# A Fourier layer in front of a mixture of experts: the first forward step in one full-precision matmul, an earlier first table, and the inverse's copies in another place of the queues

## The chip, the cores and the metric

The kernel runs on one core of one Trainium2 chip. Its time is the device time in microseconds of one execution. Five engines work side by side, each on a queue of its own that it takes in order: TensorE (PE, with its weight loads shown as PEld), VectorE (DVE), ScalarE (ACT), GpSimd (POOL) and SyncE (SP), which here only issues DMAs.

## The reference

A batch of 8 sequences of 2496 tokens of 256 numbers goes through a real Fourier transform along the sequence, a complex 256 x 256 product with a bias, a soft threshold and the inverse transform; each of the 19968 tokens then goes to the one of 8 experts that its gate scores highest.

```python
X = np.fft.rfft(x, axis=1)
Yr = Xr @ w_r - Xi @ w_i + b_r
Yi = Xr @ w_i + Xi @ w_r + b_i
Yr = np.sign(Yr) * np.maximum(np.abs(Yr) - lam, 0.0)   # Yi likewise
y = np.fft.irfft(Y, n=x.shape[1], axis=1)
# per token, with its expert e = argmax(y @ w_gate):
out = softmax(y @ w_gate)[e] * (np.maximum(y @ w1[e], 0.0) @ w2[e])
```

## The kernel before

**Numbers.** Where precision matters and speed too, a factor is split: a copy rounded to a reduced form (fp32r) on ScalarE, the rest by a subtraction on VectorE, and a product is three matmuls in the reduced form, high by high, low by high and high by low. Some matmuls take full-precision float32 instead.

**The transform** of 2496 = 39 x 64 is done in steps. The first forward step `fwd_a` (L279) multiplies a block of x by a 117 x 120 matrix of cosines and sines; a batch is 11 blocks, two for each of five x tiles and one for the sixth. Batch 0 uses float32 and one matmul a block (tile `pa`, from `x` and `far` or `fer`); the others use three, from `xh` and `xl`, which `split_x` (L269) makes. The result is copied to `ae` and stored in memory (`spec`), and `turn` (L300) loads it back turned, as `t`. Then come ten slots a batch, two frequencies of the 20 in each: `fwd_b` (L307) writes `pb`; `halves` (L317) makes `re`, `sh`, `su`, `sl` of it; `mix` (L333) makes the products `pk` and, behind it, `pm`, with `k` copied on ScalarE, `kb` added on GpSimd and `v` added on VectorE; `shrink` (L358) makes `r` on ScalarE and `y` on VectorE. The inverse of a batch runs in the slots of the next: `inv_b` (L374) makes `pv` and copies it to `z`, and `inv_a` (L387) makes `pz`, the split `zh` and `zl`, then `py`, copied to `yb`.

**The routing.** When half of a batch's `yb` is there, `route` (L558) chooses the expert of each token and its row in a sorted buffer `xs`. It is a generator: each `tick` (L519) runs it on to its next `yield`, so that its small VectorE steps are strewn over the slots. It makes a running sum, `sb`, which TensorE multiplies into `pr`; four ticks lie between them. Its rows are then scattered by GpSimd (L624), three a slot, four in the last batch, by `send` (L524). `table` (L638), also run by ticks, turns the counts into a list of tiles of 256 tokens. The first table serves the first 5 tiles, the second all others.

**The loop** is `spectral` (L411), from L454 on, over 80 slots. It enters ScalarE's and VectorE's instructions in the order written; TensorE's and SyncE's are written by hand as well. A slot `it` of batch b, slot number s, goes: `fwd_b` of the next slot, the first part of its `halves`, `r` of the slot before, the last part of `halves`, ticks, an inverse, `mix` and `fwd_a`, `y`, `split_x` for the next slot's `fwd_a`, ticks, an inverse, `y`, ticks, `pm` and `v`, an inverse, ticks, sends, DMA loads. In slots 2 to 5 of each batch but the first ("turning") three steps of `inv_a` run, one in each inverse, and `fwd_a` stands in front of `pk`; in the others the inverse is `inv_b`. `first` and `second` say which blocks a slot takes, `loads` which x tile it loads: in batch 2 and later the loads lie three or more slots ahead of use.

**Behind the loop** `finish_last` (L531) runs the last batch's `inv_a` and routing beside the first three steps of the experts (`step`, L899; `up`, L830; `down`, L859), in which `split1` and `split2` split the weights; then `experts_rest` runs the others.

Of the kernel before, what the change touches and what calls it, by code (L numbers as in the profile page):

```python
# [24 lines left out]
D = 256  # L25
# [73 lines left out]
class Kernel:  # L99
    def __init__(self, tc, nb, x, w_r, w_i, b_r, b_i, w_gate, w1, w2,  # L100
                 c_fa, c_fe, c_ga, c_bm, c_bi, c_ids, c_score, c_base, c_ltri, c_tcol, out):
        self.__dict__.update({n: v for n, v in locals().items() if n != "self"})
        self.nc = tc.nc
        self.ntok = nb * S
        self.cap = TT + self.ntok
        self.nt = (self.ntok + E * (TT - 1)) // TT
        done = (nb - 1) * S
        self.early = EARLY if done - E * (TT - 1) > (EARLY - 1) * TT else 0
        self.spec = [self.nc.dram_tensor(f"spec{i}_dram", (120, G, D), F32, kind="Internal").ap() for i in range(2)]
        self.xs = self.nc.dram_tensor("xs_dram", (E * self.cap, XW), F32, kind="Internal").ap()  # L110
# [69 lines left out]
    def open_forward(self, st):  # L180
        tc, nc, nb = self.tc, self.nc, self.nb
        f = self.f = self.pool(st, "f", 1, side="right")
        self.xp = self.pool(st, "xp", 5, side="right")
        self.tp = self.pool(st, "tp", 6, side="right")
        self.w = self.pool(st, "w", 2, side="right")
        self.psf = self.pool(st, "psf", 1, side="right", space=PSUM)

        self.far = far = f.tile([117, 120], F32, name="far")
        self.fh = f.tile([117, 120], F32R, name="fh")
        self.fl = f.tile([117, 120], F32R, name="fl")  # L190
        self.fer = f.tile([78, 120], F32, name="fer")
        self.feh = f.tile([78, 120], F32R, name="feh")
        self.fel = f.tile([78, 120], F32R, name="fel")
        nc.sync.dma_start(far, self.c_fa)
        nc.sync.dma_start(self.fer, self.c_fe)
        self.bm = f.tile([128, K1, 128], F32, name="bm")
        self.bi = f.tile([128, K1, 128], F32, name="bi")
        self.bias = f.tile([128, 2, D], F32, name="bias")
        self.xg = {}
        for q in range(6):  # L200
            self.load_x(0, q)
        nc.sync.dma_start(self.bm[:, 0:4, :], self.c_bm[:, 0:4, :])
        raw = {}
        for nm, src in (("r", self.w_r), ("i", self.w_i)):
            raw[nm] = self.w.tile([128, 2, D], F32, tag="v", name="wraw")
            nc.sync.dma_start(raw[nm], src.rearrange("(c p) n -> p c n", p=128))
        self.wh, self.wl = {}, {}
        self.raw = raw
        for h, b in ((0, self.b_r), (1, self.b_i)):
            nc.gpsimd.dma_start(self.bias[:, h, :], b.rearrange("(o n) -> o n", o=1).broadcast_to((128, D)))  # L210
        self.nlam = f.tile([128, 1], F32, name="nlam")
        nc.vector.memset(self.nlam, -LAM)

        nc.gpsimd.dma_start(self.gar, self.c_ga)
        for c in range(2):
            nc.gpsimd.dma_start(self.iw[:, c, c * 128:c * 128 + 8], self.w_gate[c * 128:(c + 1) * 128, :])
        nc.gpsimd.dma_start(self.ids, self.c_ids)
        nc.gpsimd.dma_start(self.score, self.c_score)
        nc.gpsimd.dma_start(self.base, self.c_base)
        nc.gpsimd.dma_start(self.ltri_f, self.c_ltri)  # L220
        nc.gpsimd.dma_start(self.tcol, self.c_tcol)
        nc.gpsimd.memset(self.z[:, :, 64:66, :], 0.0)
# [12 lines left out]

    def split_constants(self):
        nc, f, raw = self.nc, self.f, self.raw
        nc.scalar.copy(self.fh, self.far)
        nc.vector.tensor_sub(self.fl, self.far, self.fh)
        nc.scalar.copy(self.feh, self.fer)  # L240
        nc.vector.tensor_sub(self.fel, self.fer, self.feh)
        ws = self.w.tile([128, 2, D], F32, tag="r", name="wsum")
        wd = self.w.tile([128, 2, D], F32, tag="r", name="wdif")
        nc.vector.tensor_sub(wd, raw["i"], raw["r"])
        nc.vector.scalar_tensor_tensor(out=ws, in0=raw["i"], scalar=-1.0, in1=raw["r"], op0=ALU.mult, op1=ALU.subtract)
        raw = {"r": raw["r"], "d": wd, "s": ws}
        for nm in ("s", "d", "r"):
            self.wh[nm] = f.tile([128, 2, D], F32R, name="wh" + nm)
            self.wl[nm] = f.tile([128, 2, D], F32R, name="wl" + nm)
            nc.scalar.copy(self.wh[nm], raw[nm])  # L250
            nc.vector.tensor_sub(self.wl[nm], raw[nm], self.wh[nm])
        nc.scalar.copy(self.gh, self.gar)
        nc.vector.tensor_sub(self.gl, self.gar, self.gh)
        for c in range(2):
            nc.vector.tensor_copy(self.iw[:, c, 8 - 8 * c:136 - 8 * c], self.ident)
        nc.vector.tensor_copy(self.ltri, self.ltri_f)
# [9 lines left out]
            self.nc.sync.dma_start(t[lo * j:hi * j, :n, :].rearrange("p g d -> p (g d)"), src)  # L266
        self.xg[b, q] = t

    def split_x(self, b, q, g):  # L269
        nc = self.nc  # L270
        m = 117 if q < 5 else 78
        xt = self.xg[b, q][:m, g:g + 2, :].rearrange("p g d -> p (g d)")
        xh = self.w.tile([117, 512], F32R, tag="xh", name="xh")
        xl = self.w.tile([117, 512], F32R, tag="xl", name="xl")
        nc.scalar.copy(xh[:m, :], xt)  # L275
        nc.vector.tensor_sub(xl[:m, :], xt, xh[:m, :])  # L276
        self.xs2[b, q, g] = xh, xl

    def fwd_a(self, b, q, g):  # L279
        nc = self.nc  # L280
        m = 117 if q < 5 else 78
        raw, hi, lo = (self.far, self.fh, self.fl) if q < 5 else (self.fer, self.feh, self.fel)
        p = self.psi.tile([128, 512], F32, tag="u", name="pa", bufs=4)
        if b:
            xh, xl = self.xs2.pop((b, q, g))
            parts = ((hi, xh), (lo, xh), (hi, xl))
        else:
            parts = ((raw, self.xg[b, q][:, g:g + 2, :].rearrange("p g d -> p (g d)")),)
        for i, (a, v) in enumerate(parts):
            nc.tensor.matmul(p[:120, :], a[:m, :], v[:m, :], start=i == 0, stop=i == len(parts) - 1)  # L290
        ae = self.xp.tile([120, 2, D], F32, tag="ae", name="ae", bufs=5)
        to = ae.rearrange("p g d -> p (g d)")
        if b == 0 and g:
            nc.vector.tensor_copy(to, p[:120, :])
        else:
            with self.tc.high_priority():
                nc.scalar.copy(to, p[:120, :])
        nc.sync.dma_start(self.spec[b % 2][:, 4 * q + g:4 * q + g + 2, :], ae)
# [111 lines left out]

    def spectral(self, fwd):  # L411
        nb = self.nb
        self.t1s, self.pbs, self.ss, self.us, self.ys, self.hl, self.xs2 = {}, {}, {}, {}, {}, {}, {}
        self.jobs, self.rows = [], []
        pairs = [(q, g) for q in range(6) for g in ((0, 2) if q < 5 else (0,))]
        todo = [(b, s) for b in range(nb) for s in range(10)]
# [17 lines left out]
        for _ in self.halves(*todo[0]):  # L434
            pass

        first, second, loads, back = ({i: [] for i in range(-1, n)} for _ in range(4))
        for b in range(1, nb):
            at = 10 * b - 10
            for i, o in enumerate((1, 1, 2, 2, 3, 3, 4, 4, 5, 5, 6) if b == 1 else (-3, -2, -1, 0, 0, 1, 2, 3, 4, 5, 6)):  # L440
                first[at + o].append((b, *pairs[i]))
                second[at + o - 1].append((b, *pairs[i]))
            for q, o in enumerate((None, None, 0, 1, 1, 2) if b == 1 else (-7, -5, -4, -2, 0, 2)):
                if o is not None:
                    loads[at + o].append((b, q))
# [8 lines left out]
        for it in range(n):  # L454
            b, s = todo[it]
            late = b == nb - 1
            half, small = iter(()), iter(())
            if it + 1 < n:
                self.fwd_b(*todo[it + 1])
                half = self.halves(*todo[it + 1])  # L460
                next(half)
            if it:
                small = self.shrink(*todo[it - 1])
                next(small)
            next(half, None)
            turning = b and 2 <= s < 6
            turns = iter(range(3 * s - 6, 3 * s - 3) if turning else ())

            def inverse():
# [4 lines left out]
                    break  # L474

            spare = 1 if late else 0
            self.tick(2 + spare)
            inverse()
            mix = self.mix(b, s)
            if not turning:  # L480
                next(mix)
# [2 lines left out]
            if turning:  # L484
                next(mix)
            next(small, None)
            for a in second[it]:
                self.split_x(*a)
            self.tick(2 + spare)
            inverse()  # L490
            next(small, None)
# [8 lines left out]
                self.write_blank()  # L500
            if it + 4 < n:
                self.turn(*todo[it + 4])
            if late and self.early and s == 6:
                self.jobs.append(self.table(0))
        for _ in self.shrink(*todo[n - 1]):
            pass
# [51 lines left out]
    def route(self, b, hf, y):  # L558
# [39 lines left out]
        pa = pa[:, 8:, :]  # L598
        sb = small("sb", (117, E), BF16)
        nc.vector.tensor_copy(sb, pa[:, GH - 1, :])  # L600
        for _ in range(4):
            yield
        p = self.psi.tile([128, 512], F32, tag="yo", name="pr")
        nc.tensor.matmul(p[:117, :E], self.ltri, sb, start=True, stop=False)
# [33 lines left out]
    def table(self, last):  # L638
# [70 lines left out]
        if last:  # L709
            lap = rt.tile([128, 128], F32, name="lap")  # L710
            nc.vector.tensor_copy(lap, fin[:, 3:4].broadcast_to((128, 128)))
            yield "pe"
            p = self.psi.tile([128, 512], F32, tag="yo", name="pl")
            nc.tensor.matmul(p[:, 0:128], lap, self.ident, start=True, stop=True)
            for h in range(2):
# [253 lines left out]
```

## Time and profile before

| | us |
|---|---|
| median of 3 runs | 1668.5 (1666.49 to 1670.34) |
| the profiled execution | 1668.7 |
| its span, first to last instruction | 1666.9 |
| TensorE busy | 1534.7 (92%), 10880 instructions |
| VectorE busy | 1335.3 (80%) |
| ScalarE busy | 1116.1 (67%) |
| GpSimd busy | 617.5 (37%) |

Times in the rows count from the span's start. A matmul's record lies over the next one's, since matmuls are pipelined, so the cost of one in a row of them is read from the distance of two starts. A float32 matmul leaves two records. The granted clock (PEclk) is a share of TensorE's full speed: 1.00 is 2.4 GHz and 0.50 is 1.2 GHz, the two levels that are seen. Behind an instruction stands in brackets how long its engine stood idle before it, and for whom.

### The profile page before, as it was taken

What the parts mean: (1) busy time and instruction counts of PE and PEld (TensorE: products, weight loads), DVE (VectorE), ACT (ScalarE), POOL (GpSimd) and SP (SyncE); (2) the same over time, 40 slices, a digit from 0 to 9 for tenths busy, and PEclk for the clock granted to TensorE, in tenths of its full rate; (3) what the DMA queues carried; (4) which work ended last, traced back from release to release, by engine and by line L of the source; (5) the groups of instructions that cost most, each with busy time, mean ns of one, the idle gap of its engine ahead of it and who ended that gap; (6) DMA issues with size and microseconds to landing.
All of it is one profiled execution on the core that took longest, in us unless ns stands there. A gap on an engine that the chain in (4) does not pass through costs nothing. (4 is left out here: it accounts for less than half of the span.)

```text
span 1666.9 us, 36023 instructions
## 1 busy us (share of the span) xinstructions
PE 1534.7 (92%) x10880; PEld 1422.8 (85%) x10880; DVE 1335.3 (80%) x2755; ACT 1116.1 (67%) x2334; POOL 617.5 (37%) x462
## 2 busy tenths in 40 slices
PE   5889898988988887779999999999999999999997
PEld 2778787878878886778999999999999999999996
DVE  2678878888888888668888888888888888888886
ACT  2677777676767665546677677677677667677675
POOL 2121626362535345351333333333333333333332
PEclk8899999999999998999999999999999999999998
DMA  8753535353535311324322312312312313213210
GB/s 249 200 145 94 171 98 161 108 156 107 164 95 148 102 57 46 114 65 102 97 50 46 99 47 46 100 46 60 85 46 61 83 46 96 49 46 91 52 46 19
DMA packets 182932, 153.81 MB, mean 92 GB/s; under 512 B 120378, under 2 KB 154080, under 8 KB 182477
## 3 DMA queue, kind: packets, MB, share of 16 engines
q1 hardware_dynamic: 162829, 107.17, 25.6%
q0 software_dynamic: 19904, 44.29, 8.1%
q8 instruction: 88, 1.44, 0.4%
q14 instruction: 111, 0.91, 0.2%
HBM read 243.33 MB, written 66.37 MB: 186 GB/s over the span
## 5 line engine op out<-in xcount | busy, mean ns | idle before, releaser
L892 POOL DMA_INDIRECT out<-o,row x154 | 303.7, 1972 | 571.2 <-DVE o L890 546.1
L882 PE MATMUL po<-h,hh 128*128 128x512 f32 x1312 | 463.4, 397 | 2.7 <-ACT hh L849 2.7
L844 PE MATMUL ph<-xh,l 128*128 128x256 f32 x1312 | 372.0, 284 | 4.4 <-DVE l L785 4.4
L844 PE MATMUL ph<-xh,h 128*128 128x256 f32 x1312 | 372.4, 284 | 0.6 <-ACT h L784 0.5
L844 PE MATMUL ph<-xl,h 128*128 128x256 f32 x1312 | 371.8, 283 | 0.2 <-DVE xl L827 0.2
L849 ACT ACTIVATE hh<-ph 128x512 fp32r<-128x512 f32 x328 | 196.0, 598 | 251.9 <-PE ph L844 232.5
L850 DVE SCALAR_TENSOR_TENSOR hl<-ph,hh 128x512 fp32r<-128x512 f32 x328 | 226.7, 691 | 150.6 <-ACT hh L849 136.5
L879 PE MATMUL po<-h,hl 128*128 128x256 f32 x1148 | 322.6, 281 | 0.2 <-DVE hl L850 0.2
L882 PEld LDWEIGHTS po<-h,hh 128*128 128x128 f32 x1312 | 242.2, 189 | 47.4 <-ACT hh L849 3.0
L844 PEld LDWEIGHTS ph<-xh,l 128*128 128x128 f32 x1312 | 251.9, 192 | 8.4 <-DVE l L785 4.9
L844 PEld LDWEIGHTS ph<-xh,h 128*128 128x128 f32 x1312 | 251.4, 192 | 1.4 <-ACT h L784 0.7
L844 PEld LDWEIGHTS ph<-xl,h 128*128 128x128 f32 x1312 | 251.9, 192 | 0.4 <-DVE xl L827 0.4
L349 POOL TENSOR_TENSOR kb<-bias,k 128x512 f32<-128x512 f32 x80 | 106.1, 1326 | 332.8 <-ACT k L347 289.8
L879 PEld LDWEIGHTS po<-h,hl 128*128 128x128 f32 x1148 | 217.9, 190 | 4.5 <-DVE hl L850 0.5
L624 POOL DMA_INDIRECT xs_dram<-yb,pos x176 | 182.8, 1039 | 82.4 <-issue 43.6
L785 DVE TENSOR_TENSOR l<-r,h 128x512 fp32r<-128x512 f32 x332 | 206.8, 682 | 3.1 <-ACT h L784 3.0
L800 DVE TENSOR_TENSOR h<-r,h 128x512 fp32r<-128x512 f32 x332 | 206.9, 684 | 2.8 <-ACT h L799 2.8
L784 ACT CAST h<-r 128x512 fp32r<-128x512 f32 x332 | 180.7, 618 | 1.8 <-DMA r<-moe_w 1.8
L799 ACT CAST h<-r 128x512 fp32r<-128x512 f32 x332 | 180.4, 618 | 0.0
L368 DVE SCALAR_TENSOR_TENSOR y<-v,r 64x256 f32<-64x256 f32 x320 | 159.7, 499 | 6.1 <-issue 0.8
L381 PE MATMUL pv<-bi,y 128*128 128x128 f32 x640 | 95.3, 288 | 22.5 <-DVE y L368 20.9
L276 DVE TENSOR_TENSOR xl<-x,xh 117x512 fp32r<-117x512 f32 (+1 forms) x77 | 70.4, 926 | 56.5 <-ACT xh L275 54.7
(190 smaller groups left out, 2927.9 us busy)
## 6 DMA issues: line engine op xcount, KB each, us to landing
r<-moe_w SPq DMA_DIRECT2D x178, 512.0 KB
r<-moe_w SPq DMA_DIRECT2D x632, 128.0 KB
spec_dram<-ae SPq DMA_DIRECT2D x88, 240.0 KB
t<-spec_dram SPq DMA_DIRECT2D x160, 128.0 KB
xq<-xs_dram SPq DMA_DIRECT2D x312, 64.0 KB
x<-x SPq DMA_DIRECT2D x40, 384.0 KB
x<-x SPq DMA_DIRECT2D x40, 84.0 KB
xs_dram<-yb,pos POOLq DMA_INDIRECT x176
```

What stands on the lines that cost most here:

```text
L368: nc.vector.scalar_tensor_tensor(out=y[q * 64:q * 64 + 64, kp, :], in0=u[h, q, :], scalar=LAM, in1=r[h, q, :], op0=ALU.add, op1=ALU.min)
L624: i = nc.gpsimd.indirect_dma_start(out=self.xs[:, :], out_offset=bass.IndirectOffsetOnAxis(ap=pos[:n, g:g + 1], axis=0), in_=y[:n, g, 0:XW ...
L784: nc.scalar.copy(hi[:, c, s], v)
L785: nc.vector.tensor_sub(lo[:, c, s], v, hi[:, c, s])
L799: nc.scalar.copy(hi[:, s, :], v)
L800: nc.vector.tensor_sub(lo[:, s, :], v, hi[:, s, :])
L844: nc.tensor.matmul(p[:, i, :], a[:, c, f * 128:(f + 1) * 128], v[:, c, :], start=m == 0, stop=m == 5)
L849: nc.scalar.activation(hh[:, s, :], p, AF.Relu)
L850: nc.vector.scalar_tensor_tensor(out=hl[:, s, :], in0=p, scalar=0.0, in1=hh[:, s, :], op0=ALU.max, op1=ALU.subtract)
L879: nc.tensor.matmul(p[:, :D], hl[:, f - 1, hs], w2[:, f - 1, 0, :], start=False, stop=False)
L882: nc.tensor.matmul(p, hh[:, f, hs], w2[:, f].rearrange("p a d -> p (a d)"), start=f == 0, stop=f == 7)
L892: i = nc.gpsimd.indirect_dma_start(out=self.out[:, :], out_offset=bass.IndirectOffsetOnAxis(ap=at[h], axis=0), in_=o[:, h, :], in_offset=N ...
```

## The change

It has four parts. `split_x` and the split of the matrices go, and `fwd_a` multiplies x itself in float32 in every batch, as batch 0 does now. In turning slots the first inverse moves ahead of `r`, of the last part of `halves` and of the first ticks. `route` waits five ticks between `sb` and `pr`, and ten in the last batch. The first table is made from all batches but two and queued in slot 1 of the last batch, and the second waits three ticks more before `pl`. The `ae` tiles are eight and were five.

```diff
-        done = (nb - 1) * S
+        done = (nb - 2) * S
...
-        nc.scalar.copy(self.fh, self.far)
-        nc.vector.tensor_sub(self.fl, self.far, self.fh)
-        nc.scalar.copy(self.feh, self.fer)
-        nc.vector.tensor_sub(self.fel, self.fer, self.feh)
...
-    def split_x(self, b, q, g):
...
-        nc.scalar.copy(xh[:m, :], xt)
-        nc.vector.tensor_sub(xl[:m, :], xt, xh[:m, :])
...
     def fwd_a(self, b, q, g):
         nc = self.nc
         m = 117 if q < 5 else 78
...
-        if b:
-            xh, xl = self.xs2.pop((b, q, g))
-            parts = ((hi, xh), (lo, xh), (hi, xl))
-        else:
-            parts = ((raw, self.xg[b, q][:, g:g + 2, :].rearrange("p g d -> p (g d)")),)
-        for i, (a, v) in enumerate(parts):
-            nc.tensor.matmul(p[:120, :], a[:m, :], v[:m, :], start=i == 0, stop=i == len(parts) - 1)
-        ae = self.xp.tile([120, 2, D], F32, tag="ae", name="ae", bufs=5)
+        nc.tensor.matmul(p[:120, :], (self.far if q < 5 else self.fer)[:m, :],
+                         self.xg[b, q][:m, g:g + 2, :].rearrange("p g d -> p (g d)"), start=True, stop=True)
+        ae = self.xp.tile([120, 2, D], F32, tag="ae", name="ae", bufs=8)
...
+            turning = b and 2 <= s < 6
             if it + 1 < n:
                 self.fwd_b(*todo[it + 1])
                 half = self.halves(*todo[it + 1])
                 next(half)
-            if it:
-                small = self.shrink(*todo[it - 1])
-                next(small)
-            next(half, None)
-            turning = b and 2 <= s < 6
...
             spare = 1 if late else 0
+            if turning:
+                inverse()
+            if it:
+                small = self.shrink(*todo[it - 1])
+                next(small)
+            next(half, None)
             self.tick(2 + spare)
-            inverse()
+            if not turning:
+                inverse()
...
             next(small, None)
-            for a in second[it]:
-                self.split_x(*a)
...
-            if late and self.early and s == 6:
+            if late and self.early and s == 1:
                 self.jobs.append(self.table(0))
...
-        for _ in range(4):
+        for _ in range(10 if b == self.nb - 1 else 5):
             yield
         p = self.psi.tile([128, 512], F32, tag="yo", name="pr")
...
             nc.vector.tensor_copy(lap, fin[:, 3:4].broadcast_to((128, 128)))
-            yield "pe"
+            for _ in range(4):
+                yield
             p = self.psi.tile([128, 512], F32, tag="yo", name="pl")
```

## Rows read from the trace of the kernel before

**Rows 1.** By stretch: length, then PE, PEld, DVE, ACT, POOL busy; PEclk, DMA, GB/s.
```profile
41.60:105.80 64.20, 53.67 (x366) 49.78 (x367) 44.35 (x88) 43.21 (x93) 11.94 (x10) 0.93 0.67 187
105.80:583.60 477.80, 419.40 (x3180) 395.43 (x3179) 393.18 (x951) 337.38 (x823) 204.00 (x180) 0.97 0.44 127
583.60:666.30 82.70, 67.11 (x501) 63.59 (x500) 68.08 (x185) 46.38 (x114) 41.80 (x39) 0.92 0.17 51
666.30:700.10 33.80, 26.48 (x176) 23.46 (x175) 20.24 (x58) 20.41 (x56) 8.22 (x12) 0.90 0.42 127
700.10:764.00 63.90, 53.33 (x345) 48.23 (x344) 42.79 (x115) 30.36 (x59) 31.95 (x40) 0.92 0.22 63
764.00:1667.00 903.00, 889.87 (x6260) 833.07 (x6258) 757.51 (x1334) 629.95 (x1177) 308.19 (x158) 1.00 0.27 64
```

**Rows 2.** TensorE's waits, 105.8:583.6: total us, times, longest.
```profile
PE pr L604 <- DVE sb L600: 23.0, 6, 3.9
PE pk L341 <- ACT yb L407: 10.9, 18, 1.1
PE pv L381 <- DVE y L368: 9.9, 12, 1.6
PE pz L392 <- DVE zl L398: 7.3, 6, 1.2
```

**Rows 3.** Timeline, a plain slot: start, us, engine, line, what, idle before.
```profile
94.09 0.62 ACT L275 CAST xh<-x 117x512 fp32r<-117x512 f32 x1
94.74 0.89 DVE L276 TENSOR_TENSOR xl<-x,xh 117x512 fp32r<-117x512 f32 x1 [1.10 <-ACT xh L275]
96.57 0.71 PE L381 MATMUL pv<-bi,y 128*128 128x128 f32 x4 [0.98 <-DVE y L368]
```

**Rows 4.** Timeline, a turning slot.
```profile
209.67 0.73 ACT L362 ACTIVATE r<-v,nlam 128x512 f32<-128x512 f32 x1
211.61 0.39 PE L341 MATMUL pk<-whr,sh 128*128 128x256 f32 x1 [1.12 <-ACT yb L407]
```

**Rows 5.** Timeline, the route's sum and its matmul.
```profile
255.92 0.17 DVE L600 CAST sb<-scan 117x8 bf16<-117x8 f32 x1
256.14 0.17 PE L604 MATMUL pr<-sb,ltri 117*117 117x8 bf16 x1 [3.67 <-DVE sb L600]
```

**Rows 6.** By stretch: a plain slot, and the time behind a stall.
```profile
242.50:248.00 5.50, 5.50 (x47) 5.36 (x46) 5.12 (x18) 2.84 (x8) 2.09 (x3) 1.00 0.69 193
255.30:262.10 6.80, 5.96 (x29) 5.96 (x29) 5.21 (x14) 4.09 (x10) 4.27 (x4) 0.50 0.62 183
```

**Rows 7.** Timeline of PE and of PEld, batch 0's first step.
```profile
8.71 1.95 PE L290 MATMUL pa<-x,far 117*120 117x512 f32 x4 [0.93 <-DMA x<-x]
15.76 0.18 PEld L290 LDWEIGHTS pa<-x,far 117*120 117x120 f32 x1 [0.25 <-issue]
```

**Rows 8.** Timeline of PE, a block of batch 3.
```profile
199.61 0.40 PE L290 MATMUL pa<-xh,fl 117*120 117x512 f32 x1
199.84 0.39 PE L290 MATMUL pa<-xl,fh 117*120 117x512 f32 x1
```

**Rows 9.** TensorE's waits, 41.6:105.8.
```profile
PE pv L381 <- DVE y L368: 9.9, 8, 3.5
```

**Rows 10.** TensorE's waits, 583.6:764.
```profile
PE pr L604 <- DVE sb L600: 6.5, 2, 4.1
PE ph L844 <- DVE l L785: 4.0, 1, 4.0
PE pq L706 <- DVE fin L700: 2.9, 1, 2.9
PE pl L714 <- DVE lap L711: 2.1, 1, 2.1
```

**Rows 11.** Groups of the page: count, busy us, mean ns, idle before.
```profile
L349 POOL TENSOR_TENSOR kb<-bias,k 128x512 f32<-128x512 f32 x80 | 106.1, 1326 | 332.8 <-ACT k L347 289.8
L624 POOL DMA_INDIRECT xs_dram<-yb,pos x176 | 182.8, 1039 | 82.4 <-issue 43.6
```

More of the change, by code (lines that the diff above doesn't have):

```diff
@@ L188, in open_forward @@
         self.far = far = f.tile([117, 120], F32, name="far")
-        self.fh = f.tile([117, 120], F32R, name="fh")
-        self.fl = f.tile([117, 120], F32R, name="fl")
         self.fer = f.tile([78, 120], F32, name="fer")
-        self.feh = f.tile([78, 120], F32R, name="feh")
-        self.fel = f.tile([78, 120], F32R, name="fel")
         nc.sync.dma_start(far, self.c_fa)
@@ L267, in load_x @@
         self.xg[b, q] = t
-    def split_x(self, b, q, g):
[L270 to L274, printed above, removed]
-        nc.scalar.copy(xh[:m, :], xt)
-        nc.vector.tensor_sub(xl[:m, :], xt, xh[:m, :])
-        self.xs2[b, q, g] = xh, xl
     def fwd_a(self, b, q, g):
@@ L281, in fwd_a @@
         m = 117 if q < 5 else 78
-        raw, hi, lo = (self.far, self.fh, self.fl) if q < 5 else (self.fer, self.feh, self.fel)
         p = self.psi.tile([128, 512], F32, tag="u", name="pa", bufs=4)
-        if b:
-            xh, xl = self.xs2.pop((b, q, g))
-            parts = ((hi, xh), (lo, xh), (hi, xl))
-        else:
-            parts = ((raw, self.xg[b, q][:, g:g + 2, :].rearrange("p g d -> p (g d)")),)
-        for i, (a, v) in enumerate(parts):
-            nc.tensor.matmul(p[:120, :], a[:m, :], v[:m, :], start=i == 0, stop=i == len(parts) - 1)
-        ae = self.xp.tile([120, 2, D], F32, tag="ae", name="ae", bufs=5)
+        nc.tensor.matmul(p[:120, :], (self.far if q < 5 else self.fer)[:m, :],
+                         self.xg[b, q][:m, g:g + 2, :].rearrange("p g d -> p (g d)"), start=True, stop=True)
+        ae = self.xp.tile([120, 2, D], F32, tag="ae", name="ae", bufs=8)
         to = ae.rearrange("p g d -> p (g d)")
@@ L412, in spectral @@
         nb = self.nb
-        self.t1s, self.pbs, self.ss, self.us, self.ys, self.hl, self.xs2 = {}, {}, {}, {}, {}, {}, {}
+        self.t1s, self.pbs, self.ss, self.us, self.ys, self.hl = {}, {}, {}, {}, {}, {}
         self.jobs, self.rows = [], []
@@ L435, in spectral @@
             pass
-        first, second, loads, back = ({i: [] for i in range(-1, n)} for _ in range(4))
+        first, loads, back = ({i: [] for i in range(n)} for _ in range(3))
         for b in range(1, nb):
@@ L441, in spectral @@
                 first[at + o].append((b, *pairs[i]))
-                second[at + o - 1].append((b, *pairs[i]))
             for q, o in enumerate((None, None, 0, 1, 1, 2) if b == 1 else (-7, -5, -4, -2, 0, 2)):
```

## The prediction

> **What bounds the kernel now.** I read the busy time by stretch first [rows 1]. From 764 us to the end TensorE is busy for 889.9 of 903.0 us at a granted clock of 1.00: the change has no instruction there, and nothing can be won there by easing another engine. Everything lies ahead of it. In 105.8:583.6, which is six batches of ten slots, TensorE is busy 419.4 of 477.8 us, VectorE 393.2, ScalarE 337.4. None is full, so order and waiting set the time: TensorE's queue is in order and stands for 58.4 us, and its mean clock of 0.97 costs 0.03 x 477.8 = 14.3 us more.
>
> The second view is who TensorE waits for in that stretch [rows 2]. The matrix for the prefix sums, pr, waits for VectorE's sb 6 times, once a batch, for 23.0 us; pk waits for yb 18 times, 10.9 us; pv waits for y 12 times, 9.9 us; pz waits for zl 6 times, 7.3 us. Together 51.1 of the 58.4 us. The third view is the timeline at each of them. A plain slot [rows 3]: ScalarE's split xh starts at 94.09, VectorE's xl has stood 1.10 us for it and runs to 95.63, the y behind it comes that much later, and TensorE's pv stands 0.98 us for y. So the split of x is in the loop: a copy on one engine, then a subtraction at the head of the other's queue, in front of y. A slot that turns a batch back [rows 4]: r starts at 209.67 on ScalarE and stands in front of zh and yb, which the next pk waits for (1.12 us). The route [rows 5]: sb ends at 256.09, pr starts at 256.14 after 3.67 us, and from 255.3 to 262.1 the granted clock is 0.50 [rows 6], the lower of its two levels. The mean of 0.97 is what six such drops, one behind each pr wait, leave.
>
> **Part 1, full precision without a split.** It removes 77 xh from ScalarE (0.62 us each) and 77 xl from VectorE (0.89 in the row) [rows 3], and three TensorE matmuls a block for one in full precision. Its price stands in batch 0, which works so already: a block is two records, as four of them for the two blocks of one x take 1.95 us with their tail [rows 7], and their weight loads come every 0.43 us (the one at 15.76: 0.18 behind 0.25 of standing), so a block is 0.86 us. Now a block is three records, 0.23 us apart (199.61, 199.84) [rows 8], 0.69 us. So +0.17 us x 77 = +13.1 us of TensorE's own time, with no cover, since TensorE is what I expect to be late everywhere: 14 blocks up to 105.8 (2.4 us), 63 behind (10.7 us). Bounds for a block: 0.86 from the spacing, 0.98 from half of the 1.95; I take 0.86, as the spacing repeats and the tail overlaps what follows.
>
> The Trainium skill's page FP8 and Floating Point Precision (TensorE Precision Notes) says that true FP32 takes four passes through the array, against the three matmuls here. An estimate by that page is 4 x 0.23 = 0.92 us a block and +17.7 us in all; the trace has 3.7 times the reduced one, and the sum goes by the trace.
>
> The matmul now waits for x itself, on TensorE, where ScalarE waited a slot earlier; x is issued over three slots ahead in all batches but the first two, so I cost this at nothing. In batch 1 it lands late; pv's longest wait for y, 3.5 us, is in that stretch [rows 9]. If x were later than the matmul, pk and pm would be queued behind it. x's buffers come free one slot later; from batch 2 on each is loaded again three or more slots behind its last use, so SP's queue does not stand. Three more ae buffers: at nothing.
>
> **Part 2, the inverse first.** In slots 2 to 5 the first inverse goes in front of r, sh's last part and the tick. Nothing is added; r, and y behind it, come later by two zh and two yb, under 1.9 us, since r, sh, both zh and both yb all lie between 209.67 and 211.61 [rows 4]. This is covered: y is used by pv not before the next slot, and v by pm later still. What goes: most of pk's 10.9 and pz's 7.3 us. Next to be late is VectorE, whose zl now comes in front of the last sl.
>
> **Part 3, the route.** It has one tick more between sb and pr, but in the turning slots a route is also queued before the first tick, not behind it. Counting calls: sb was call 8 in the first tick of slot 8, pr call 12 in its third; now sb is call 8 in the last tick of slot 7, and pr call 13, again in the third of slot 8. So pr keeps its place and sb comes ahead of a whole set of su, sl, y. With xl gone in front of it as well, I expect no wait there, and with the wait the six drops of the clock go. In the last batch pr goes six ticks later instead.
>
> **Part 4, the table.** It is queued in slot 1 of the last batch, not 6; its VectorE steps and two TensorE groups move from slots 77 and 78 to 72 and 73, and pl moves three ticks later. Five early tiles remain (6 x 2496 - 8 x 255 is far over 1024). SP's queue is not moved: the weights behind it wait for the forward pools.
>
> **The sum, by stretch** [rows 1, 2, 9, 10].
> 41.6:105.8: pv <- y stands 9.9 us; I leave 1. Of the clock's 0.07 x 64.2 = 4.5 us I count 1.5, since most lies at the start, which stays. Less 2.4: a gain of 8.
> 105.8:583.6: 58.4 + 14.3 = 72.7 us are to be had, I leave 8 (some 1.3 us a batch of the waits that I count away), less 10.7: a gain of 54. Ends: 62 if nothing is left; 37 if half of the 35.4 us that are not pr's stays, and half of the clock's.
> 583.6:666.3: idle 15.6, clock 0.08 x 82.7 = 6.6. VectorE is busy 68.1 of 82.7 us, so at most 14.6 can go; pq's 2.9 us go for sure, as the table leaves this place. The other waits (pr's longest, 4.1 us, among them) hang on a full VectorE, into which the table now falls at slots 72 and 73. I take the middle, 9.
> 666.3:700.1: pr's other wait is 6.5 - 4.1 = 2.4 us, the clock's share 0.10 x 33.8 = 3.4. Six ticks are a tile and a half of the inverse: both go nearly wholly. 5, ends 0 and 5.8.
> 700.1:764: idle 10.6, clock 5.1. pl's 2.1 us go; of ph <- l, 4.0 us, half, as the table's steps leave that place in VectorE's queue; one drop of the clock, 1.7. But route and table now run into the next step of the experts, in front of its hl: 1 to 4.0 us new (the same row is the bound). 5, ends -4 and 10.
> Together 8 + 54 + 9 + 5 + 5 = 81 us. The profiled execution took 1668.7 us (span 1666.9), the median is 1668.5, so the two can be taken as one: 1668.7 - 81 = 1588 us.
>
> **Rivals.**
> The pr wait stays. If VectorE comes to sb as late as before (the route's small steps and the scatters beside them are all still there), 23.0 us and the clock's 14.3 stay, and the time is 1588 + 37 = 1625. For it: sb was over 3.6 us late, and one xl is 0.89 us. Against: two xl and their waits for xh stand in front of sb, and sb itself moves ahead.
> POOL becomes the bound of the plain slots. A slot has three scatters of 1.04 us and one kb of 1.33 us [rows 11], and 43.6 / 176 = 0.25 us of issue ahead of a scatter, 5.2 us together; a plain slot that TensorE fills is 5.5 us long now [rows 6]. If POOL sets the six plain slots of a batch, at 0.5 us more each than TensorE would, that is 18 us: 1606. Against: kb is needed only after the next pm, so some lateness is free. The skill's page SBUF (SBUF: two separate sides) says that VectorE and GpSimd lock a shared port pair for a whole instruction; denser slots would raise that, and no run here shows by how much.
> Slower: the matmul in full precision falls on TensorE and the split was not what it waited for. Then the waits stay, since the loop closes through r, z, k and kb, which no part shortens, and 13.1 us come on top: 1682. It decides where less than 13.1 of the 72.7 + 14.4 us in the first two stretches come back. Against: rows 3 show xl in front of y.
> The change does not do what it says: here that would be a route whose calls I miscounted, which is the first rival.
>
> **How the numbers follow.** The forecast has 0.60 (1568 to 1610 by itself, with its ends not all on one side), the pr wait 0.18, POOL 0.16, slower 0.04, and 0.02 for gains that cancel. The range runs from 1568 to 1626 and takes in the first two rivals' times. About 0.2% (3.3 us) is what a measurement of this kernel can tell from no change: faster 0.94, same 0.02, slower 0.04.
>
> **What would show it.** Right: 0.86 us a block; no L275 and L276; TensorE's waits for sb gone between 105.8 us and the last batch, and a clock of 1.00 there; a batch in 70 to 71 us where it took 477.8 / 6 = 79.6; pk and pz without waits for yb and zl. Wrong: a batch still over 74 us with waits for kb or v (POOL), or for sb; blocks over 1 us; new waits of TensorE for x, or for hl and l in the first three steps of the experts.

## The result, and the profile after

The changed kernel takes 1605.16 us (median of 4 runs, 1603.11 to 1609.34) against 1669.42 for the kernel before on the same chip: a ratio of 0.9619, with a 95% interval of 0.9592 to 0.9646. It is 64 us faster, where 81 were forecast, and lies inside the range of 1568 to 1626. The profiled execution took 1606.7 us, its span 1604.9.

By stretch (the columns are those of [rows 1]), cut at the first `pb` of slots 0, 10, 70 and 78 and at the first `ph` of steps 0 and 3 of the experts:

```profile
40.60:93.00 52.40, 52.40 (x352) 45.34 (x353) 42.33 (x76) 35.20 (x79) 13.28 (x10) 0.95 0.77 223
93.00:533.80 440.80, 418.00 (x3116) 380.81 (x3115) 377.46 (x887) 307.21 (x759) 203.63 (x180) 0.98 0.47 138
533.80:604.50 70.70, 55.95 (x425) 52.68 (x424) 58.91 (x168) 38.97 (x99) 32.23 (x30) 0.93 0.16 48
604.50:647.60 43.10, 36.04 (x262) 33.35 (x261) 28.81 (x73) 28.85 (x73) 16.77 (x17) 0.92 0.39 119
647.60:690.90 43.30, 38.81 (x268) 34.41 (x266) 35.41 (x108) 22.26 (x44) 31.88 (x37) 1.00 0.22 70
690.90:1604.90 914.00, 900.36 (x6324) 842.87 (x6324) 765.25 (x1345) 636.47 (x1189) 310.94 (x162) 0.99 0.26 65
```

| stretch | before, us | after, us | gain | forecast |
|---|---|---|---|---|
| ahead of slot 0 | 41.6 | 40.6 | 1.0 | 0 |
| slots 0 to 9 | 64.2 | 52.4 | 11.8 | 8 |
| the sixty slots | 477.8 | 440.8 | 37.0 | 54 |
| slots 70 to 77, and the tail | 66.6 + 51.3 | 70.7 + 43.1 | 4.1 | 14 |
| steps 0 to 2 | 53.8 | 43.3 | 10.5 | 5 |
| the rest | 911.6 | 914.0 | -2.4 | 0 |
| span | 1666.9 | 1604.9 | 62.0 | 81 |

The tail is slots 78 and 79 and what follows up to the first step of the experts. The forecast's own cuts lie up to 9 us away from these behind slot 77, so the last rows are compared only roughly. The largest shortfall is one term: 17 us in the sixty slots. Slots 70 to 77 with the tail fall 10 us short, and slots 0 to 9 and the steps together make up 9. TensorE's waits in the sixty slots (total us, times, longest), against [rows 2]:

```profile
PE pr L580 <- DVE scan L570: 11.7, 6, 3.0
PE py L382 <- ACT k L323: 5.7, 6, 1.9
PE py L382 <- DVE zl L374: 2.5, 6, 0.4
PE pv L357 <- DVE y L344: 1.5, 3, 0.7
PE pk L317 <- ACT yb L383: 0.9, 1, 0.9
```

The waits of pz, pk and pv, 28.1 us before, are down to 2.4. The route's pr still waits once a batch, 11.7 us where it was 23.0, and py now waits for k, which it did not. The timeline around one pr (start, us, engine, line, what; in brackets the idle time before it):

```profile
148.01 0.28 ACT L550 ACTIVATE ex<-lg 117x88 f32<-117x88 f32 x1 [3.02 <-DVE mx L547]
151.08 1.83 DVE L344 SCALAR_TENSOR_TENSOR y<-v,r 64x256 f32<-64x256 f32 x2
151.33 1.29 POOL L325 TENSOR_TENSOR kb<-bias,k 128x512 f32<-128x512 f32 x1 [1.50 <-ACT k L323]
154.08 0.93 DVE L344 SCALAR_TENSOR_TENSOR y<-v,r 64x256 f32<-64x256 f32 x2
156.63 0.17 DVE L576 CAST sb<-scan 117x8 bf16<-117x8 f32 x1
156.85 0.17 PE L580 MATMUL pr<-sb,ltri 117*117 117x8 bf16 x1 [1.74 <-DVE scan L570]
```

Two suspects stand in it. ScalarE stood 3.02 us in front of `ex`, the route's exponential, since its input comes from VectorE; re, sh and r of the next slot are queued behind. And the pair of `y` beside GpSimd's `kb` took 1.83 us, ending at 152.91 just behind kb's end at 152.62, where the next pair took 0.93. Theory A says that the place of ex holds the loop up; theory B that kb holds VectorE up.

### The profile page after: what moved, and what is told of

Its sections match the earlier page's. It is cut to its first block, busy times and chain, and to the rows that moved or that the text cites. A ratio compares the mean times of both kernels' runs of the same rounds, so it can differ in the third digit from the quotient of the medians.

```text
span 1604.9 us, 35620 instructions
## 1 busy us (share of the span) xinstructions
PE 1523.7 (95%) x10803; PEld 1398.7 (87%) x10803; DVE 1317.3 (82%) x2676; ACT 1077.0 (67%) x2255; POOL 620.1 (39%) x460
## 5 line engine op out<-in xcount | busy, mean ns | idle before, releaser
L325 POOL TENSOR_TENSOR kb<-bias,k 128x512 f32<-128x512 f32 x80 | 111.2, 1390 | 292.5 <-ACT k L323 222.0
L344 DVE SCALAR_TENSOR_TENSOR y<-v,r 64x256 f32<-64x256 f32 x320 | 187.9, 587 | 6.0 <-ACT r L338 1.6
L289 PE MATMUL pb<-bm,t 128*128 128x128 f32 x640 | 90.3, 287 | 12.8 <-DMA t<-spec_dram 10.5
L368 PE MATMUL pz<-iw,z 128*120 128x136 f32 x704 | 98.6, 284 | 0.7 <-issue 0.7
```

Source lines behind the costliest of these rows:

```text
L344: nc.vector.scalar_tensor_tensor(out=y[q * 64:q * 64 + 64, kp, :], in0=u[h, q, :], scalar=LAM, in1=r[h, q, :], op0=ALU.add, op1=ALU.min)
```

## Experiments

### Part 1 alone

> The kernel before with part 1 alone (float32 first step, no split of x, eight ae tiles). Theory: the split stood in the loop of the plain slots, so the first ten slots fall from 64.2 to about 52.5 us and pv's waits for y in the sixty slots behind them go (9.9 us); pr's wait for sb shrinks from 3.8 us a batch but stays, since sb keeps its place. Sixty slots: 477.8 to about 448. In all about 1627. Rival (the wait for sb and the turning slots carry the change, the split was cover): sixty slots over 465, in all 1645 or more. A float32 block is 0.86 us by both.

The edit: of the change only the full-precision `fwd_a`, without `split_x`, and the eight ae buffers. Measured: 1615.59 us, ratio 0.9688 (0.9671 to 0.9704). So part 1 brings some 52 of the 64 us. The sixty slots take 436.8 us; TensorE's waits in them:

```profile
PE pr L577 <- DVE sb L573: 12.5, 6, 3.4
PE pk L317 <- ACT yb L383: 10.0, 18, 1.6
```

It is 11 us better than expected, and so are the sixty slots. The waits for y and zl went with the split; pr's wait was nearly halved by it, before part 3 did anything. Parts 2 to 4 give nothing more in this stretch, which takes 440.8 us after, and 435.2 us in another execution of the same sixty slots (the run with the table in slot 6, below).

### The change without part 1

> The changed kernel with part 1 undone: x is split again, the other three parts stay. Theory: the first ten slots are back at 64 us, plain slots at 5.4 to 5.9 us, and pr waits for sb longer than the 1.7 us of the changed kernel, about 2.5 us a batch, with the drops of the clock; the turning slots keep most of their gain (39.2 us a batch before, 36 now). In all about 1640. Rival (part 1 gives little): within 10 us of the changed kernel's 1605.

The edit: `split_x` and the three matmuls a block put back into the changed kernel. Measured: 1646.98 us, 0.9885 (0.9862 to 0.9908). The rival that expected no difference falls. Slots 0 to 9 take 62.2 us, nearly the 64.2 of before, and in the sixty slots (469.5 us) pv waits for y again:

```profile
PE pv L381 <- DVE y L368: 14.4, 12, 1.6
```

The 52 us of part 1 alone and the 20 of the rest alone are more than the 64 of both: the parts take some of the same waits away.

### The change without part 2

> The changed kernel with part 2 undone: r and the rest stand in front of the first inverse in the turning slots again. Theory: the four turning slots of a batch go from 36 us back to about 38.5, as pk waits for yb and pz for zl again, over seven batches 15 to 20 us: 1622. The routes start two ticks later, so sb and pr both move later; the wait stays at 1 to 2 us a batch. Rival (part 1 alone freed the turning slots): within 5 us of 1605.

```diff
-            if turning:
-                inverse()
             if it:
                 small = self.shrink(*todo[it - 1])
                 next(small)
             next(half, None)
             self.tick(2 + spare)
-            if not turning:
-                inverse()
+            inverse()
```

Measured: 1613.48 us, 0.9676 (0.966 to 0.9693): part 2 is worth some 9 us, half of what was expected. Little of it lies where it was expected: the sixty slots take 442.8 us, 2 more than in the changed kernel, while slots 70 to 77 take 74.2 against 70.7. The waits in the sixty slots say why:

```profile
PE pk L317 <- ACT yb L383: 9.5, 18, 1.7
PE pv L357 <- DVE y L344: 9.1, 5, 1.8
PE pr L577 <- DVE sb L573: 4.2, 6, 1.8
```

Without part 2, part 3's extra tick works: pr waits 4.2 us where part 1 alone left 12.5. With part 2 it is back at 11.7, and py <- k is new. What part 2 takes away in this stretch comes back there: TensorE is idle for 24.1 us without it and 22.8 with it. The inverse in front of the first ticks also lets a route start two ticks earlier, and with it goes ex.

### The first table in slot 6 again

> The changed kernel with the first table queued in slot 6 of the last batch again, as before. Theory: slot 72 (16.1 us in the changed kernel, with a wait of 5.6 us for zl behind the table's VectorE steps and a drop of the clock) falls to about 10 us, and the table's matmuls at the end of the loop stand again for 3 to 4 us with a drop. The place is worth little either way: 1600 to 1608. Rival (slot 72 is long because of the scatters and y): slot 72 stays over 14 us, and the time is 1610 or more.

```diff
-            if late and self.early and s == 1:
+            if late and self.early and s == 6:
```

Measured: 1601.68 us, 0.9599 (0.9583 to 0.9616), not separable by time from the changed kernel (0.9592 to 0.9646). The stretches say more. Slot 72 of the changed kernel, then that of this one:

```profile
543.00:559.10 16.10, 8.56 (x65) 8.00 (x64) 12.93 (x51) 5.41 (x16) 10.35 (x10) 0.86 0.27 82
```
```profile
538.90:548.10 9.20, 7.91 (x65) 7.39 (x64) 6.82 (x15) 4.45 (x14) 7.77 (x8) 1.00 0.38 114
```

In the changed kernel the table's small steps, from 549.00 us on, stand in front of a zl on VectorE, and one of 128x4 lies beside a kb (start, us, engine, line, what):

```profile
550.86 1.95 DVE L626 TENSOR_TENSOR pfb<-pfa 128x4 f32<-128x4 f32 x1
551.48 1.29 POOL L325 TENSOR_TENSOR kb<-bias,k 128x512 f32<-128x512 f32 x1
558.05 0.58 PE L382 MATMUL py<-zl,gh 120*117 120x272 f32 x1 [5.60 <-DVE zl L374]
```

Slots 70 to 77 take 66.0 us here, 70.7 in the changed kernel; tail and steps take 90.1, there 86.4. So the early table gives 3.7 us behind and costs 4.7 where it lands.

This run also shows how far one execution stands from the next. Up to slot 70 its program is that of the changed kernel, and TensorE is idle for as long (22.6 us against 22.8), yet the sixty slots take 435.2 us:

```profile
92.70:527.90 435.20, 412.58 (x3117) 375.12 (x3116) 374.87 (x883) 305.31 (x756) 201.21 (x179) 0.99 0.48 139
```

What differs is TensorE's clock: it stands at 0.50 for 20.4 us of them in the execution of the changed kernel, and for 6.8 us here. The next run, again the same program up to slot 70, takes 436.4 us for them, also with 6.8 us at 0.50. So differences of 5 us between two stretches of sixty slots can be the clock alone.

### The last batch's longer waits taken back

> The changed kernel with the last batch's ten ticks back to five, and the three ticks ahead of pl taken out; the early table and all else stay. If these ticks give the tail's and the steps' gain (11.2 and 5.9 us against the kernel with part 1 alone), it is lost again: 1618 to 1623 us. If the early table gives it: within 5 us of 1605.

```diff
-        for _ in range(10 if b == self.nb - 1 else 5):
+        for _ in range(5):
...
-            for _ in range(4):
-                yield
+            yield
```

Measured: 1608.83 us, 0.9658 (0.9628 to 0.9688). The larger loss does not come: the tail keeps its gain (43.5 us), and only the steps lose 5. In tail and steps three waits are back that the changed kernel has not:

```profile
PE pr L580 <- DVE sb L576: 2.4, 1, 2.4
PE ph L820 <- DVE l L761: 2.3, 1, 2.3
PE pl L690 <- DVE tab L684: 1.2, 1, 1.2
```

With the late table and the ten ticks tail and steps are 90.1 us, with the early table and five ticks 91.8, with both 86.4, with neither (part 1 alone, so without part 2 as well, its table made from all batches but one) 103.4. Either gives most of the gain, so it can't be put down to one.

### Theory A: the exponential one tick later

> The changed kernel, with the route's exponential ex on ScalarE entered one tick later and its input kept in a tile of its own, so that ScalarE no longer stands for VectorE's mx and lg (3.02 us and 1.21 us a time in the trace of after). Theory A (where ex now falls in ScalarE's queue is what leaves TensorE waiting for sb and for k): the waits pr <- VectorE (8.7 us) and py <- k (5.7 us) between 93 and 518 us go, with a clock drop or two: 1586 to 1592 us. Theory B (GpSimd's kb holds VectorE up, 48 us of stretched steps in the sixty slots, and ex's place is free): within 5 us of 1605, the waits for VectorE stay.

```diff
         ex = small("ex")
+        yield
         nc.scalar.activation(ex, lg, AF.Exp)
-        yield
         first, odd, even = self.scan
+        sg = small("sg")
...
-        nc.vector.scalar_tensor_tensor(out=lg, in0=lg, scalar=0.0, in1=self.score[:, hf * GH:(hf + 1) * GH, :],
+        nc.vector.scalar_tensor_tensor(out=sg, in0=lg, scalar=0.0, in1=self.score[:, hf * GH:(hf + 1) * GH, :],
...
```

The steps behind then read sg in place of lg. Measured: 1592.39 us, 0.9545 (0.9519 to 0.9571): faster than the changed kernel, with intervals that do not meet, and 0.4 us above the range that theory A gave. The sixty slots, and TensorE's waits in them:

```profile
97.80:522.70 424.90, 409.22 (x3116) 372.09 (x3115) 376.82 (x883) 306.33 (x756) 200.68 (x179) 1.00 0.49 143
```
```profile
PE pv L357 <- DVE y L344: 3.8, 6, 0.9
PE py L382 <- DVE zl L374: 2.7, 7, 0.4
PE pr L581 <- DVE scan L571: 2.7, 4, 0.7
PE pr L581 <- issue: 2.4, 1, 2.4
```

py <- k is gone, pr waits 5.9 us with what is not shown here, and the clock is 1.00. Theory A holds in this: the waits that it named are gone or halved. The stretch is 15.9 us shorter than the changed kernel's 440.8, of which 7.1 are idle time and the rest the clock, and 10.3 shorter than the 435.2 us with the table in slot 6; by the ratios of all runs the edit gives 12 us. The tile of its own had no wait to take away: in the changed kernel VectorE stood 0.0 us in front of the step that may not overwrite lg before ex has read it. That leaves 15.7 us of idle TensorE.

### Theory B: without kb

> The changed kernel without GpSimd's kb: the bias is left out, v adds k itself, and a GpSimd copy of one element keeps the place of the scatters. Theory B: the steps of VectorE that were stretched beside kb (52 of them, 48 us over their medians in the sixty slots) take their medians, TensorE's waits for VectorE in 93:518 (13.6 us with scan, zl, y and yb) go, and the time is 1582 to 1592 us, the sixty slots under 425. Theory A: VectorE has time to spare anyway, ScalarE still stands for mx, py still waits for k: over 1598 us.

```diff
-        kb = self.w.tile([128, 2, D], F32, tag="kb", name="kb", bufs=1)
-        self.paced = nc.gpsimd.tensor_tensor(out=kb, in0=self.bias, in1=k.unsqueeze(1).broadcast_to((128, 2, D)), op=ALU.add)
+        self.pace(k[0:1, 0:1], always=True)
...
-        nc.vector.tensor_add(u, p, kb)
+        nc.vector.tensor_add(u, p, k.unsqueeze(1).broadcast_to((128, 2, D)))
```

Measured: 1611.03 us, 0.9673 (0.9642 to 0.9703). `pace` is the GpSimd copy of one element. This looks like the end of theory B, and is a flaw of the edit. There is one tile `k`; with v reading it, ScalarE may not write the next k before v is done. A new wait comes with it, and is gone again in the next run:

```profile
PE pz L367 <- DVE zl L373: 12.8, 4, 3.7
```

So it was made again with two k tiles.

> The changed kernel without GpSimd's kb and without the bias, as before, but with two k tiles, so that ScalarE's next k does not wait for v. Theory B, with the tie through k taken out: VectorE's 48 us of stretching and most of TensorE's waits go, 1582 to 1594 us. Theory A: the stretched steps lie where VectorE has room, py <- k and pr <- VectorE stay: 1598 to 1610 us.

```diff
-        k = self.w.tile([128, D], F32, tag="k", name="k", bufs=1)
+        k = self.w.tile([128, D], F32, tag="k", name="k")
```

Measured: 1559.33 us, 0.9389 (0.9373 to 0.9406). Taking kb away is worth 2.3% or 38 us. The sixty slots, in which pr waits 1.1 us and py for k still 4.6:

```profile
95.20:504.80 409.60, 403.88 (x3117) 371.53 (x3116) 320.94 (x887) 306.98 (x759) 134.38 (x178) 1.00 0.51 148
```

But this also shortens the path from k to v by 1.4 us of kb. The run that tells the two apart computes kb and lets nobody read it:

> The kernel without the bias and with two k tiles (no_kb2), but with GpSimd's kb computed as in the changed kernel, from the bias and k, and read by nobody: v still adds k itself. So the path from k to v is as short as in no_kb2, and GpSimd reads SBUF as long as in the changed kernel (about 1.39 us a slot). If what kb costs is that VectorE's steps stand still beside it, nearly all of the 46 us between no_kb2 (1559) and the changed kernel (1605) come back: 1592 to 1606 us, with some 48 us of stretched VectorE steps in the sixty slots. If it is the longer path from k over kb to v: 1558 to 1566 us. In between, the share of each can be read.

The edit: no_kb2's two k tiles and its v, with the changed kernel's kb left in place. Measured: 1607.41 us, 0.9624 (0.9604 to 0.9644), that is the changed kernel's time again. The run without kb has the same values and the same routing, the bias being left out of both, so the two differ only in this addition and the copy of one element that stands for it: 0.9389 against 0.9624, 39 us. The length of the path from k to v is worth nothing, and no engine waits for GpSimd in the sixty slots of this run, so it isn't GpSimd's longer queue either. What costs is that GpSimd does this addition beside VectorE. VectorE's `y` (count, busy us, mean ns, idle before) without kb, then with the unread one:

```profile
L343 DVE SCALAR_TENSOR_TENSOR y<-v,r 64x256 f32<-64x256 f32 x239 | 100.0, 418 | 3.3
```
```profile
L344 DVE SCALAR_TENSOR_TENSOR y<-v,r 64x256 f32<-64x256 f32 x237 | 141.4, 596 | 3.3
```

### Both theories at once, and two versions that keep the bias

> Both, exponential one tick later and no kb, no bias, two k tiles. If, with ex out of the way, what kb holds up is what TensorE waits for next (15.7 us idle in the sixty slots of ex3), the sixty slots come down to 410 to 416 us and the time to 1576 to 1586. If not, within 4 us of ex3's 1592.

Measured: 1551.34 us, 0.9337 (0.9318 to 0.9356). Less than expected was left over: TensorE is idle for 0.2 us in sixty slots. By the ratios the two edits give 12 and 38 us one at a time and 47 together, so they relieve nearly separate waits.

```profile
91.90:494.40 402.50, 402.29 (x3117) 371.31 (x3116) 320.14 (x887) 308.40 (x759) 134.60 (x178) 1.00 0.52 151
```

> The changed kernel with kb on VectorE, read straight from pk's bank, and k's copy on ScalarE gone. VectorE gets 0.68 us more a slot (41 us in sixty slots), ScalarE 0.45 less, GpSimd 1.35 less. Theory B: about 48 us of stretching go for these 41, evenly spread where the stretching came in lumps beside the route, and py no longer waits for k (5.7 us): 1592 to 1602 us. Theory A: VectorE gets 41 us and gains nothing: 1605 to 1625 us.

The edit: kb is a VectorE addition of pk's bank and the bias, entered ahead of the second inverse; k's copy goes. Measured: 1615.28 us, 0.968 (0.9651 to 0.9709), not the gain that theory B named but inside theory A's range, though y is stretched no more (418 ns in the mean) and VectorE's busy time falls from 377.5 to 357.7 us. A new wait takes the place of the old ones, three times a batch: TensorE's py waits for ScalarE's yb. Why yb is late there was not followed.

```profile
PE py L382 <- ACT yb L383: 18.9, 18, 1.6
```

> The changed kernel with the exponential one tick later (as in ex3) and the first table queued in slot 6 of the last batch (still made from all batches but two). The two gains lie in different stretches, 12.8 us for ex3 and 3.5 us for the later table by their medians, so if each is what it was taken for the time is 1586 to 1591 us, with slot 72 near 9 us and the sixty slots near 425. If both relieve the same wait: 1592 or more.

The edit: theory A's, and the table in slot 6. Measured: 1583.61 us, 0.954 (0.952 to 0.9561). The kernel before took 1661.05 us in that comparison, so the ratio counts, and it is that of theory A's edit alone (0.9545). These two keep the whole computation and beat both kernels of this case; that the later table adds anything is not shown.

## Why the prediction was right, and where it was off

**The price of a block: right.** A full-precision block starts at 246.62; behind it the weight loads come 0.43 us apart, as in [rows 7], and from 247.49 on they keep their usual pace. That is 0.87 us, where 0.86 was taken. A plain slot with a block that TensorE filled before and after (slot number 7 of five batches) went from 5.53 to 5.67 us, 0.14 where 0.17 was said.

```profile
246.62 1.02 PE L265 MATMUL pa<-x,far 117*120 117x512 f32 x2
247.06 0.19 PEld L317 LDWEIGHTS pm<-whd,sh 128*128 128x128 f32 x1 [0.25 <-issue]
247.49 0.19 PEld L317 LDWEIGHTS pm<-wld,sh 128*128 128x128 f32 x1 [0.24 <-issue]
```

**The split was in the loop: right.** Part 1 alone gives 52 us, and the change without it 20. In slots 0 to 9 TensorE is busy for all of 52.40 us; the forecast had left 1 us of waits and 3 of the clock's 4.5 there, and the gain is 11.8 where 8 was said. The rival "slower" falls.

**The sixty slots: the step that was mis-sized.** The forecast was 415.8 us of TensorE's own time and 8 us left of waits and clock. By the row above, 440.8 - 418.0 = 22.8 us of waits and 0.02 x 440.8 = 8.8 of the clock are left, 31.6 us, and the own time is 409.2. The left-over term was short by 23.6 us, and the own time was 6.6 too long: with no waits at all it is 402.3 (the row of both theories at once), so the 419.4 us of [rows 1] held time, beyond the clock's, that goes when the waits go. The two errors make the 17. In the two other executions of the same program the left-over is smaller by the clock, 27 us (22.6 of waits and 0.01 x 435.2 of the clock) and 28, and still more than three times what was said. Its signs are mixed: a batch takes 73.5 us, between the 70 to 71 named for right and the 74 named for wrong, the wait of pr is not gone, and the clock is not 1.00.

**Why so much was left.** Two claims failed.
First, of part 3: "I expect no wait there". The working followed one of the route's calls, sb, from slot to slot, and not call 2, ex, on the other engine. ex had moved ahead of re, sh and r on ScalarE, where it stands for VectorE: 25.4 us in the sixty slots, against 18.8 in the kernel before. Moving it a tick on makes the stretch 10 to 16 us shorter. Without part 2, ex stands for 1.27 us in the same place of the trace, behind that work and not ahead of it.
Second, that xl's 0.89 us a block goes from VectorE. It goes, 60.5 us in the sixty slots of before, but VectorE's busy time falls from 393.2 to 377.5 only. These are its groups before:

```profile
L368 DVE SCALAR_TENSOR_TENSOR y<-v,r 64x256 f32<-64x256 f32 x240 | 119.1, 496 | 3.4
L276 DVE TENSOR_TENSOR xl<-x,xh 117x512 fp32r<-117x512 f32 x57 | 51.7, 915 | 40.6 <-ACT xh L275 38.8 <-ACT ae L297 1.3
L594 DVE TENSOR_TENSOR scan<-scan 117x88 f32<-117x88 f32 x48 | 11.8, 246 | 1.0
L276 DVE TENSOR_TENSOR xl<-x,xh 78x512 fp32r<-78x512 f32 x6 | 8.8, 1473 | 1.4 <-ACT xh L275 1.4
L613 DVE TENSOR_TENSOR lg<-scan,rb 117x88 f32<-117x88 f32 x12 | 3.9, 324 | 0.2
```

and after:

```profile
L344 DVE SCALAR_TENSOR_TENSOR y<-v,r 64x256 f32<-64x256 f32 x239 | 140.8, 589 | 3.3
L570 DVE TENSOR_TENSOR scan<-scan 117x88 f32<-117x88 f32 x48 | 18.2, 378 | 1.1
L589 DVE TENSOR_TENSOR lg<-scan,rb 117x88 f32<-117x88 f32 x12 | 8.9, 743 | 0.2
```

The same y, scan and lg take (140.8 + 18.2 + 8.9) - (119.1 + 11.8 + 3.9) = 33.1 us more. xl of 78 rows took 1473 ns, xl of 117 rows 915: one and a half times as long for fewer rows can't be the work itself. All six of the first kind overlap a kb of GpSimd and end behind it; this is one in the kernel before:

```profile
232.63 1.38 POOL L349 TENSOR_TENSOR kb<-bias,k 128x512 f32<-128x512 f32 x1 [8.79 <-ACT k L347]
233.10 1.45 DVE L276 TENSOR_TENSOR xl<-x,xh 78x512 fp32r<-78x512 f32 x1 [0.25 <-ACT xh L275]
```

So xl was a step that stood beside kb; with it gone, y and the route's steps stand there. This could have been read in the kernel before. How the two failures share pr's and py's waits can be read from the runs: py <- k goes with ex's place (5.7 to 0 us) and hardly with kb (4.6), pr's wait halves with ex's place (11.7 to 5.9) and nearly goes with kb (1.1).

The prediction named the Trainium skill for it, page SBUF — State Buffer, and wrote that no run shows by how much. The page's section Who interferes with whom goes further: a VectorE instruction with two SBUF inputs contends with a GpSimd instruction that reads SBUF. y, scan, lg and xl are of that kind, and the runs agree: kb beside VectorE costs 38 us of the kernel's time. SBUF is the memory that holds these tiles; pz, TensorE's output, lies elsewhere, so zl has one input there, and its mean is the same with kb as without (433 and 436 ns). A step with a single input, which this sentence does not cover, is stretched as well: mx of 117x11 takes 610 ns in the mean with kb and 191 without.

**The rival of GpSimd: the right engine by another way.** Its 1606 us was all but met, by luck: TensorE waits neither for kb nor for v in the sixty slots, VectorE's v waits for kb once, 1.3 us, and the rival's own sum, 5.2 us of GpSimd in a slot of 5.5, never gave the 0.5 us a slot that it charged. GpSimd costs by what it does to VectorE's steps, not by its own length. The rival of the pr wait was half right: 11.7 of 23.0 us stay.

**Part 2: right in what goes, short in what comes.** pk <- yb goes, 10.9 us before and 0.9 after (pz <- zl goes with part 1 already). "This is covered" was nearly true of r and y (pv <- y is 1.5 us), but the route's first tick, behind the inverse now, brought ex to another place.

**The last batch and the steps: nearly right together (14.6 for 19), not apart.** The table in slots 72 and 73 was counted inside a gain; it made slot 72 16.1 us long. Behind, pq's and pl's waits go as said, ph <- l too, and the expected ph <- hl comes (2.3 us).

**What stays open.** "The rest" is 2 to 7 us longer in all changed versions. In the changed kernel most of its 2.4 us is the clock, which stands at 0.50 from 691.0 to 694.4 us, behind a wait of 1.8 us for h in front of the first matmul of step 3; the kernel before has no fall there. Why h is late was not tried. And no version was found that takes kb off GpSimd, keeps the bias and gains by it.

## What to carry to other kernels

Before an operation is struck from an engine's bill, look at its mean duration beside that of its neighbours: where a smaller tile takes longer, the engine may be standing inside the instruction for another engine, and here that time passed on to what came in its place. When work made of several calls is moved, follow each call on every engine's queue, not only the one that TensorE waits for. And to tell an engine's interference from a dependency, compute the suspected value and let nobody read it.

## What the runs showed of the hardware

An addition of 128x512 on GpSimd (kb, 1.3 to 1.4 us) makes a VectorE step of 128x4 last 1.95 us, where its like of 128x7 just before took 0.16, and a pair of y 1.83 instead of 0.93. Scatters from GpSimd don't stretch y: with all of them kept and kb gone, y's mean is 418 ns. A few small steps they do: without kb, the carry_b of 117x8 takes 0.38 us beside a scatter (at 159.55 us) and 0.17 elsewhere.

TensorE's clock falls behind waits of the same length in one place and not in another. These are the 3.4 us behind two waits of pr, of 1.74 us each, in one execution of the changed kernel, and then those behind the first of the two in the run with the table in slot 6, whose program is the same up to there:

```profile
157.00:160.40 3.40, 3.40 (x32) 3.40 (x31) 3.34 (x7) 3.24 (x8) 1.46 (x1) 1.00 0.17 49
230.20:233.60 3.40, 3.40 (x19) 3.40 (x18) 3.31 (x8) 2.89 (x7) 1.79 (x2) 0.50 0.20 48
```
```profile
157.90:161.30 3.40, 3.40 (x19) 3.40 (x18) 3.31 (x9) 3.13 (x8) 2.46 (x2) 0.50 0.38 86
```

So a wait that is left costs its length and, in some executions, about half of such a stretch more. With theory A's edit, whose waits in the sixty slots are 2.4 us at most and mostly under 1, the clock stays at 1.00 throughout them.
